# A spectral mixer with two MLP layers: the transforms of three of four batches on quarters of the array, and new places for the operands

## The chip, the core and the metric

One core of a Trainium2 chip (trn2). A time is the device time of one execution in microseconds (us); the kernel before took 1374.87 us, the median of three runs (1373.92 to 1375.44). A profile is one execution taken by the hardware profiler.

## The reference

Four batches of 3136 tokens with 256 features pass through three stages (`x` float32, everything in float32):

```
X = rfft(x, axis=tokens);  y = irfft(X * (filt_r + 1j*filt_i))          # a global filter
m = real(fft(fft(y, axis=tokens), axis=features)); u = y + m            # Fourier mixing
un = (u - mean(u)) / sqrt(var(u) + 1e-6)
v = u + max(un @ w_ch1, 0) @ w_ch2                                      # layer 1, 256 -> 1024 -> 256
vn = (v - mean(v)) / sqrt(var(v) + 1e-6) * g_ln
out = v + max(vn @ w_ch1', 0) @ w_ch2'                                  # layer 2
```

## The kernel before, in words

**Transforms.** 3136 = 64 x 49, so a transform over tokens is one over 64 (index p) and one over 49 (index q), without twiddle factors. `over_p(b)` (L346) multiplies the tokens of a batch by the 64-point matrix `f1`: a chunk holds two blocks of 256 features, a block holds two q of 64 p, and `f1` is block-diagonal, 128 x 128. The products (64 real numbers per q: 32 frequencies, real and imaginary) go to DRAM (`g_dram`). `over_q(b)` (L393) reads them back with q and real/imaginary on 98 partitions, two of the 33 frequencies per step (17 steps, `XCH`), multiplies by the 49-point matrix `f2` (128 columns), multiplies by the filter (L455 to L463, with real and imaginary halves on partitions 0 to 63 and 64 to 127), goes back with `i1` (L475), and stores to `v_dram`. On the way it makes the spectrum of the filtered signal (`z`, L498) and transposes it (L479); from it comes the mixing term. `prep_ticks(U)` (L561) makes a unit U of four tiles of 128 tokens: the mixing (L592) and the last 64-point product `i2` (L606) accumulate in one bank, even and odd parts apart, and `token` (L594) makes sum and difference.

**Exact and split products.** The matrix engine has two ways here. An exact product takes float32 operands (L309). A split product (`mm3`, L219) uses float32r operands, each split into a high and a low part (ScalarE makes the high part, L224, GpSimd or VectorE the low one, L225), in three passes. Before, batch one, the first eight chunks (`N1`) of `over_p(1)` and unit 0 are exact; the rest of the transforms, the mixing and the layers are split.

**Layers.** `w1_step` (L761) multiplies 128 of the 1024 hidden features (six matmuls of 512 columns; weights stationary, `xt` moving), `w1_evict` (L776) makes `hh` and `hl` from the bank, `w2_step` (L788) accumulates the second product (twelve matmuls of 256 columns; `hh`, `hl` stationary, weights moving). A block is eight such steps of one unit and layer, 50 blocks are 400 steps.

**Order.** The order is written out by hand: each generator (`over_p`, `over_q`, `prep_ticks`, `ln_ticks`, `conv_ticks`) yields ticks, and a table puts ticks at steps of the layers (`at`, `PAIRS`, `P1`, `CONV`). An engine executes its instructions in program order. The main loop (L988 to L999) does `w1_step` of two steps ahead, the ticks of this step, `w2_step`, `w1_evict`. Batch one is transformed ahead of the first layer step (`DURING`, `AFTER`), together with the decoding of the weights (`conv_ticks`) and the first part of batch two. SP issues nearly all loads, ScalarE the stores of `g_dram` and `v_dram`. PSUM has 8 banks of 128 x 512 in one pool.

**Places.** Tiles of a pool lie one behind the other in SBUF, rounded up to 32 bytes a partition, pools in the order in which they are made (L161 to L181).

Of the kernel before, what the change touches and what calls it, by code (L numbers as in the profile page):

```python
# [9 lines left out]
F32 = mybir.dt.float32  # L10
# [9 lines left out]
NP, NQ = 64, 49  # L20
# [3 lines left out]
NV = 4 * NH  # L24
NJ = 25
KK = [0, 32] + list(range(1, 32))
NK = len(KK)
NT = B * S // 128
NU = 6 * B


CN = ["f1", "f2", "f2a", "f2b", "i1", "i1a", "i1b", "i2", "cs0", "cs0b", "cs1", "cs1b", "id"]
CI = {n: i * 128 for i, n in enumerate(CN)}
NCONST = len(CN) * 128 + 2 + NK + D + 128

# [13 lines left out]
def _consts():  # L49
    c = np.zeros((128, NCONST))  # L50
    p = np.arange(NP)
# [5 lines left out]
    f1 = np.zeros((NP, 2, 32))  # L57
    f1[:, 0, :] = c64[:, :32]
    f1[:, 1, 1:] = -s64[:, 1:32]
    f1[:, 1, 0] = c64[:, 32]  # L60
    f1 = f1.reshape(NP, 64)
# [6 lines left out]
    for h in range(2):  # L68
        r = slice(64 * h, 64 * h + 64)
        c[r, CI["f1"] + 64 * h:CI["f1"] + 64 * h + 64] = f1  # L70
        c[r, CI["i2"] + 64 * h:CI["i2"] + 64 * h + 64] = i2


# [9 lines left out]
    for n, m in (("f2", f2), ("f2a", f2a), ("f2b", f2b)):  # L83
        c[:98, CI[n]:CI[n] + 128] = m.reshape(98, 128)


    h49 = slice(0, NH)
    i1 = np.zeros((2, 64, 2, NH, 2))
    i1[0, :NQ, 0, :, 0] = c49[:, h49]
    i1[0, :NQ, 0, :, 1] = s49[:, h49]  # L90
    i1[1, :NQ, 1, :, 0] = -s49[:, h49]
    i1[1, :NQ, 1, :, 1] = c49[:, h49]
# [5 lines left out]
    for n, m in (("i1", i1), ("i1a", i1a), ("i1b", i1b)):  # L98
        c[:, CI[n]:CI[n] + NV] = m.reshape(128, NV)

# [7 lines left out]
    c[:, CI["cs0"]:CI["cs0"] + 256] = cs0  # L108
    c[:, CI["cs1"]:CI["cs1"] + 256] = cs1
    c[:, CI["id"]:CI["id"] + 128] = np.eye(128)  # L110

    o = len(CN) * 128
    c[:64, o] = 1.0
    c[64:, o] = -1.0
    c[0, o + 1] = 1.0
    c[1:, o + 1] = -1.0
    k = _crt()[np.array(KK)]
    sg = np.where(k == 0, 0, np.where(k < S // 2, 1, np.where(k == S // 2, 0, -1)))

    f2s = -f2[:, :, ::-1]  # L120
    c[:98, NCONST - 128:] = f2s.reshape(98, 128)
    c[:NQ, o + 2:o + 2 + NK] = sg.T
    c[64:64 + NQ, o + 2:o + 2 + NK] = -sg.T
    for r in (0, 64):
        c[r, o + 2 + NK:o + 2 + NK + D] = np.where(e % 2, -1, 1)
    return c.astype(np.float32)

NA, LAG = 3, 3  # L130
N1 = 8
AHEAD = 3
# [939 lines left out]
```

## Time and profile before

| | |
|---|---|
| median of three runs | 1374.87 us |
| span of the profiled execution, first to last instruction | 1372.8 us |
| what lies around the span, against the median | 2.1 us |
| TensorE matmul busy | 1346.0 us, 98% |
| VectorE, ScalarE, GpSimd busy | 890.3, 746.7, 411.0 us |
| DMA | 157.06 MB, mean 114 GB/s |

The profile gives no time of its own for the profiled execution beside its span; the span stands for it. PE is the matrix engine (TensorE) and PEld its weight load, DVE is VectorE, ACT ScalarE, POOL GpSimd, SP the engine that issues DMAs. L221 is line 221 of the kernel. Matmuls are pipelined: a record's duration includes the time through the array, and the distance from one start to the next is shorter. An exact matmul instruction leaves two records, a split pass one.

### The profile page before, as it was taken

The page shows a single profiled execution, that of the slowest core. Times are in us where ns is not written, and L with a number is a line of the kernel's source. Part 1 is how long each engine was busy: PE and PEld are TensorE (multiplying, and loading weights), DVE is VectorE, ACT ScalarE, POOL GpSimd, SP SyncE. Part 2 cuts the span into 40 slices and gives each one's busy share as a digit, 9 for nine tenths or more (in the row PEclk, how much of TensorE's full clock was granted, in tenths as well). Part 3 has the DMA queues.
Part 4 walks back from the last instruction along what each step waited for, and adds up shares of the span by engine and source line. Part 5 has one row for each costly group of instructions (what it writes and reads, how often), then busy time and mean ns, then how long its engine had stood idle before and what let it go on. Part 6 is the DMA issues. An engine that isn't in the chain of part 4 may idle for free.

```text
span 1372.8 us, 23348 instructions
## 1 busy us (share of the span) xinstructions
PE 1346.0 (98%) x8619; PEld 1192.2 (87%) x8619; DVE 890.3 (65%) x1742; ACT 746.7 (54%) x1529; POOL 411.0 (30%) x358
## 2 busy tenths in 40 slices
PE   8978999999999999999999999999999999999998
PEld 6547898888889989898899998898999999999998
DVE  5978887787555767877554667678555555555353
ACT  5665555666555665656446556566534444454322
POOL 1742134545332433534043344344111101101000
PEclk9999999999999999999999999999999999999999
DMA  8872324354435534624544544445222413422200
GB/s 303 283 227 100 102 82 120 119 154 118 133 110 146 151 87 136 179 68 121 121 129 126 144 114 144 111 134 131 65 62 47 92 32 70 85 78 46 62 16 24
DMA packets 224338, 157.06 MB, mean 114 GB/s; under 512 B 164352, under 2 KB 187904, under 8 KB 224224
## 3 DMA queue, kind: packets, MB, share of 16 engines
q1 hardware_dynamic: 208272, 132.37, 35.0%
q10 hardware_dynamic: 15952, 23.20, 5.3%
q8 instruction: 68, 1.11, 0.3%
q14 instruction: 46, 0.38, 0.1%
HBM read 99.83 MB, written 55.71 MB: 113 GB/s over the span
## 4 chain that ended last, share of the span: by engine, by line
PE 87%; DVE 6%; ACT 2%; DMA 2%; issue 2%; POOL 1%; SPq 0%; ACTq 0%; DVEq 0%; POOLq 0%
PE ps L799 36%; PE ps L771 36%; PE ps L221 8%; PE ps L592 2%; PE ps L309 1%; DVE t L460 1%; PE ps L326 1%; DVE xtl L690 1%; PE ps L479 1%; DVE y L455 1%; POOL y L462 1%; PE ps L447 1%; DVE hl L782 1%; DVE nb L648 0%; PE ps L696 0%
## 5 line engine op out<-in xcount | busy, mean ns | idle before, releaser
L782 DVE SCALAR_TENSOR_TENSOR hl<-ps,hh 128x512 fp32r<-128x512 f32 (+1 forms) x400 | 270.4, 677 | 286.2 <-ACT hh L781 281.5
L781 ACT ACTIVATE hh<-ps 128x512 fp32r<-128x512 f32 (+1 forms) x400 | 232.9, 585 | 325.0 <-PE ps L799 310.5
L771 PE MATMUL ps<-xth,w1a 128*128 128x512 f32 (+1 forms) x800 | 244.6, 387 | 0.0
L771 PE MATMUL ps<-xth,w1b 128*128 128x512 f32 (+1 forms) x800 | 243.8, 386 | 0.0
L799 PEld LDWEIGHTS ps<-w2b,hh 128*128 128x128 f32 x1568 | 208.9, 188 | 13.2
L799 PE MATMUL ps<-w2a,hh 128*128 128x256 f32 x1568 | 217.0, 281 | 0.4 <-ACT hh L781 0.4
L799 PE MATMUL ps<-w2b,hh 128*128 128x256 f32 x1568 | 217.0, 281 | 0.0
L799 PEld LDWEIGHTS ps<-w2a,hh 128*128 128x128 f32 x1568 | 206.9, 189 | 11.4 <-ACT hh L781 0.9
L644 POOL TENSOR_TENSOR rs<-rs,mhalf 128x4 f32<-128x4 f32 (+1 forms) x51 | 50.7, 994 | 376.3 <-DVE rs L643 263.5
L771 PE MATMUL ps<-xtl,w1a 128*128 128x512 f32 (+1 forms) x400 | 156.5, 391 | 2.0 <-DVE xtl L690 2.0
L771 PE MATMUL ps<-xtl,w1b 128*128 128x512 f32 (+1 forms) x400 | 155.8, 390 | 0.2 <-DVE xtl L699 0.2
L771 PEld LDWEIGHTS ps<-xth,w1a 128*128 128x128 f32 x800 | 135.7, 188 | 17.2 <-ACT xth L224 0.2
L771 PEld LDWEIGHTS ps<-xth,w1b 128*128 128x128 f32 x800 | 135.2, 188 | 16.5
L655 ACT ACTIVATE xn<-u,nb,rs 128x256 f32<-128x256 f32 x152 | 120.0, 839 | 53.0 <-DVE nb L648 53.0
L462 POOL TENSOR_TENSOR y<-y,t 128x512 f32<-128x512 f32 (+1 forms) x67 | 98.3, 1467 | 144.4 <-DVE t L460 112.4
L799 PE MATMUL ps<-w2b,hl 128*128 128x256 f32 x784 | 122.4, 277 | 1.2 <-DVE hl L782 1.2
L799 PE MATMUL ps<-w2a,hl 128*128 128x256 f32 x784 | 122.5, 278 | 1.1 <-DVE hl L782 1.1
L799 PEld LDWEIGHTS ps<-w2b,hl 128*128 128x128 f32 x784 | 103.9, 188 | 2.0 <-DVE hl L782 2.0
L799 PEld LDWEIGHTS ps<-w2a,hl 128*128 128x128 f32 x784 | 104.4, 189 | 1.3 <-DVE hl L782 1.3
L225 POOL TENSOR_TENSOR sl<-gr,sh 98x512 fp32r<-98x512 f32 x48 | 62.1, 1294 | 141.5 <-ACT sh L224 141.5
L803 DVE TENSOR_TENSOR u<-ps,u 128x512 f32<-128x512 f32 x98 | 63.2, 686 | 46.7 <-PE ps L799 46.7
L771 PEld LDWEIGHTS ps<-xtl,w1a 128*128 128x128 f32 x400 | 75.3, 188 | 19.0 <-DVE xtl L690 4.1
(132 smaller groups left out, 2053.8 us busy)
## 6 DMA issues: line engine op xcount, KB each, us to landing
fc<-in_ff SPq DMA_DIRECT2D x61, 512.0 KB
xd<-xn SPq DMA_DIRECT2D x38, 512.0 KB
xtl<-xd SPq DMA_DIRECT2D x152, 128.0 KB
vd<-vst ACTq DMA_DIRECT2D x64, 200.0 KB
xr<-in_x SPq DMA_DIRECT2D x48, 256.0 KB
vr<-vd SPq DMA_DIRECT2D x48, 256.0 KB
out<-u SPq DMA_DIRECT2D x24, 512.0 KB
gr<-gd SPq DMA_DIRECT2D x48, 196.0 KB
```

What stands on the lines that cost most here:

```text
L221: nc.tensor.matmul(out=o, lhsT=lhs[a], rhs=rhs[b], start=start and i == 0, stop=stop and i == 2)
L225: (lo_eng or nc.vector).tensor_tensor(out=lo, in0=src, in1=f32(hi), op=ALU.subtract)
L309: nc.tensor.matmul(out=o, lhsT=cf[i // 512][:k, i % 512:i % 512 + w], rhs=rhs[:k, c0:c1], start=start, stop=stop)
L462: (nc.gpsimd if b or t < n - 1 else nc.vector).tensor_tensor(out=y[:, :nk], in0=y[:, :nk], in1=t2[:, :nk], op=ALU.add)
L592: nc.tensor.matmul(out=o, lhsT=lhs, rhs=rhs[r], start=i == 0, stop=False)
L644: nc.gpsimd.tensor_tensor(out=rs[:, tl], in0=rs[:, tl], in1=mhalf[:, tl], op=ALU.pow)
L655: nc.scalar.activation(out=xs[t], in_=u[:, t].rearrange("p (k a j) -> p j k a", k=2, j=4), func=ACTF.Identity, scale=rs[:, t:t + 1], bias= ...
L771: nc.tensor.matmul(out=o, lhsT=w[:, a, k, m * 128:m * 128 + 128], rhs=xt[s][:, k, :n], start=i == 0, stop=i == 5)
L781: nc.scalar.activation(out=h[:, :n], in_=ps[:, :n], func=ACTF.Relu)
L782: nc.vector.scalar_tensor_tensor(out=l[:, :n], in0=ps[:, :n], scalar=0.0, in1=f32(h[:, :n]), op0=ALU.max, op1=ALU.subtract)
L799: nc.tensor.matmul(out=o[:, t % 2], lhsT=a[:, t * 128:t * 128 + 128], rhs=w[:, b, m], start=m == 0 and i == 0 and t % 2 == 0, stop=m == 7 ...
L803: nc.vector.tensor_tensor(out=u[:, t - 1:t + 1], in0=o, in1=u[:, t - 1:t + 1], op=ALU.add)
```

## The change

1. Batches two to four are folded ahead: the host lays token block q and block 49 - q side by side, GpSimd makes their sum and difference (`fold`). The 49-point transforms then have 50 rows (25 cosine, 25 sine) and each product is one of a 64-row, 64-column quarter of the array, in exact float32 (`quarter`). Nothing of batches two to four is split any more, in `over_p`, `over_q` or the product `i2` of `prep_ticks`; the mixing and the layers stay split.
2. Real and imaginary parts lie in different banks (R, I), and the two halves of the partitions hold two frequencies, so the filter takes four multiplications and two GpSimd additions for four frequencies; the half spectrum `z` moves from VectorE to GpSimd. `over_q` has 9 double steps (`NDUO`) instead of 17, `over_p` 7 chunks instead of 13. The filter of these batches is loaded once per frequency and not twice; `v_dram` has 128 rows per frequency instead of 100.
3. Batch one keeps its full-array exact products, in a function of its own (`first_q`) with the same arithmetic. Of the constants only the cosines and sines of the mixing are split now.
4. The pools are put in another order with gaps (`PAD`, in words of 4 bytes) between them, so that the operands of the layers start at chosen places modulo 256 bytes.
5. The tables of ticks change (`DURING`, `AFTER`, `P1`, `PAIRS`); loads of x come in chunks of 512 KB.

```
+PAD = (24, 16, 56, 40, 16, 8, 40)
-PAIRS = [(4, 5), (10, 11), (0, 1), (2, 3), (12, 14), (6, 8)]
+PAIRS = [(6, 7), (12, 13), (1, 2), (10, 11), (14, 15), (3, 5)]
...
+    sm = pool("sm", 4)
+    head = pool("head", 1)
+    gap("gap0", PAD[0])
     keep = pool("keep", 1)
+    gap("gap1", PAD[1])
+    keep64 = pool("keep64", 1)
+    uop = pool("uop", 1)
+    gap("gap2", PAD[2])
+    wp1 = pool("wp1", 1)
+    gap("gap3", PAD[3])
+    wp2 = pool("wp2", 1)
...
+    gap("gap5", PAD[5])
     xtp = pool("xtp", 2)
+    gap("gap6", PAD[6])
     hp = pool("hp", 2)
...
+    def quarter(o, c, lhs, r, k, rhs, **kw):
+        nc.tensor.matmul(out=o[c:c + 64], lhsT=lhs[r:r + k], rhs=rhs[r:r + k], **{"start": True, "stop": True, **kw})
...
+    def fold(b, c, minus):
+        t = x_raw.pop((b, c))
+        if c == 6:
+            return t
+        xf = raw.tile([128, 2, 2, D], F32, tag="xf", name="xf")
+        nc.gpsimd.tensor_tensor(out=xf[:, 0], in0=t[:, 0::2], in1=t[:, 1::2], op=ALU.add)
+        minus.tensor_tensor(out=xf[:, 1], in0=t[:, 0::2], in1=t[:, 1::2], op=ALU.subtract)
+        return xf
...
+    def over_p(b):
...
+        for c in range(7):
+            cur = xf
+            if c + 1 < 7:
+                xf = fold(b, c + 1, nc.gpsimd)
...
+                ps = [bank() for _ in range(2)]
+                for g in range(2):
+                    for h in range(2):
+                        quarter(ps[h], 64 * g, const("f1", 64 * g, 64), 64 * h, 64, flat(cur[:, g]))
...
+        def into(j):
+            g = g_raw.pop((b, j))
+            R, I = (bank(2) for _ in range(2))
...
+                n = len(steps_of(j))
+                for c in range(2):
+                    for r, o in ((0, R), (64, I)):
+                        quarter(o[:, :n], 64 * c, f2, r, NI, g[:, c:2 * n:2])
+        def filt(j, R, I):
...
+            for o, i, a in ((y[:, :n, 0], R, 0), (t2[:, :n, 1], R, 1), (y[:, :n, 1], I, 0), (t2[:, :n, 0], I, 1)):
+                nc.vector.tensor_tensor(out=o, in0=i[:, :n], in1=f[:, :n, a], op=ALU.mult)
+            nc.gpsimd.tensor_tensor(out=y[:, :n, 1], in0=y[:, :n, 1], in1=t2[:, :n, 1], op=ALU.add)
+            nc.gpsimd.tensor_tensor(out=y[:, :n, 0], in0=y[:, :n, 0], in1=t2[:, :n, 0], op=ALU.subtract)
+        def half(j):
...
+            for r, op in ((0, ALU.add), (1, ALU.subtract)):
+                eng.tensor_tensor(out=z[:, :n, r, 1:], in0=y[:, :n, r, 1:128], in1=y[:, :n, r, 129:], op=op)
+        def back(j):
...
+                for c in range(2):
+                    for h in range(2):
+                        quarter(V[h][:, :n], 64 * c, const("i1", 64 * c, 64), 64 * h, NQ, y[:, :n, c])
...
+        for j in range(NDUO + lag):
+            RI = into(j) if j < NDUO else None
+            if j >= lag:
+                back(j - lag)
+            if RI:
+                filt(j, *RI)
+            yield
+            if j >= lag:
+                turn_z(j - lag)
...
-            for a in range(2):
-                ps = bank(2)
-                for eo in (1, 0):
-                    mix(ps[:, eo], a, eo)
-                    mm3(ps[:, eo], con("i2"), cols(vs[eo], a * D, a * D + D), start=False)
...
+        for eo in (1, 0):
+            for a in range(2):
+                for h in range(2):
+                    quarter(ps[a][:, eo], 64 * (h ^ a), const("i2"), 64 * h, 64, vs[eo][:, a], start=False,
+                            stop=eo == 0, skip_group_check=True)
```

Three double steps differ from what is quoted: in the first (frequencies 0, 32 and 1) `into` has eight quarters of 256 columns and `back` six, in the last each has four of 256 columns; in `over_p` the seventh chunk has two quarters of 256 columns.

## Rows read from the trace of the kernel before

**Rows 1.** The page's header, busy times, and granted clock by slice of the span
```profile
span 1372.8 us, 23348 instructions
...
PE 1346.0 (98%) x8619; PEld 1192.2 (87%) x8619; DVE 890.3 (65%) x1742; ACT 746.7 (54%) x1529; POOL 411.0 (30%) x358
...
PEclk9999999999999999999999999999999999999999
```

**Rows 2.** The page's chain that ended last, shares of the span
```profile
PE 87%; DVE 6%; ACT 2%; DMA 2%; issue 2%; POOL 1%; SPq 0%; ACTq 0%; DVEq 0%; POOLq 0%
PE ps L799 36%; PE ps L771 36%; PE ps L221 8%; PE ps L592 2%; PE ps L309 1%; DVE t L460 1%; PE ps L326 1%; DVE xtl L690 1%; PE ps L479 1%; DVE y L455 1%; POOL y L462 1%; PE ps L447 1%; DVE hl L782 1%; DVE nb L648 0%; PE ps L696 0%
```

**Rows 3.** Waits of TensorE: total us, times, longest
```profile
PE ps L326 <- DMA xr<-in_x: 4.2, 1, 4.2
PE ps L696 <- ACT xn L661: 3.2, 6, 1.3
...
PE ps L771 <- DVE xtl L699: 0.2, 1, 0.2
```

**Rows 4.** Busy time by stretch (engines in the header line), all; then L221 alone
```profile
core 0: us, PE busy (x) PEld busy (x) DVE busy (x) ACT busy (x) POOL busy (x), PEclk, DMA share, GB/s
...
200.00:950.00 750.00, 747.69 (x4816) 670.75 (x4815) 509.58 (x961) 447.24 (x934) 290.46 (x245) 1.00 0.46 127
...
0.00:94.00 94.00, 0.00 (x0) 0.00 (x0) 1.00 0.78 270
...
200.00:950.00 750.00, 121.67 (x537) 87.51 (x537) 1.00 0.46 127
950.00:1372.00 422.00, 21.47 (x114) 16.61 (x114) 1.00 0.25 57
sum 1372.00, PE 153.86 PEld 112.30; mean PE 38.47 PEld 28.07
```

**Rows 5.** Timeline of TensorE: start, duration, instructions; split products, then a layer step
```profile
611.24 0.40 PE L221 MATMUL ps<-sh,chi 98*128 98x512 f32 x1
...
612.42 0.39 PE L221 MATMUL ps<-sl,chi 128*100 128x512 f32 x1
612.65 0.38 PE L479 MATMUL ps<-ctail,z 128*128 128x128 f32 x2
...
614.24 0.62 PE L771 MATMUL ps<-xth,w1b 128*128 128x512 f32 x2
...
615.62 0.28 PE L799 MATMUL ps<-w2b,hh 128*128 128x256 f32 x1
```

**Rows 6.** Timeline of TensorE, a unit's mixing and last transform
```profile
635.41 0.28 PE L592 MATMUL ps<-chi,zsh 128*128 128x256 f32 x1
...
636.83 1.07 PE L799 MATMUL ps<-w2a,hh 128*128 128x256 f32 x8
```

**Rows 7.** Timeline of TensorE, exact products of batch one
```profile
36.83 1.02 PE L447 MATMUL ps<-gr,f2s 98*128 98x512 f32 x2
37.69 1.02 PE L309 MATMUL ps<-y,cr 128*100 128x512 f32 x2
38.55 0.38 PE L479 MATMUL ps<-ctail,z 128*128 128x128 f32 x2
```

**Rows 8.** Groups by form of TensorE: count, busy us, mean ns, idle before
```profile
L221 PE MATMUL ps<-sl,chi 128*128 128x256 f32 x99 | 28.1, 284 | 1.8 <-DVE sl L225 1.8
...
L221 PE MATMUL ps<-sh,chi 128*100 128x512 f32 x45 | 18.1, 401 | 0.0
...
L221 PE MATMUL ps<-sh,chi 128*128 128x512 f32 x28 | 11.4, 407 | 0.0
...
L309 PE MATMUL ps<-xr,cr 128*128 128x512 f32 x16 | 7.9, 597 | 1.1 <-DMA xr<-in_x 1.1
L221 PE MATMUL ps<-sl,chi 98*128 98x256 f32 x9 | 2.5, 283 | 0.0
```

**Rows 9.** Timeline of TensorE, two layer steps late in the span
```profile
1202.44 1.09 PE L799 MATMUL ps<-w2a,hh 128*128 128x256 f32 x8
```

**Rows 10.** Groups by form: splits and additions on GpSimd and ScalarE
```profile
L462 POOL TENSOR_TENSOR y<-y,t 128x512 f32<-128x512 f32 x63 | 95.1, 1509 | 142.2 <-DVE t L460 112.4 <-ACT xth L685 15.5 <-DVE t L457 9.8
...
L225 POOL TENSOR_TENSOR sl<-gr,sh 98x512 fp32r<-98x512 f32 x48 | 62.1, 1294 | 141.5 <-ACT sh L224 141.5
...
L224 ACT ACTIVATE sh<-gr 98x512 fp32r<-98x512 f32 x48 | 29.9, 622 | 0.0
```

**Rows 11.** Groups by form: the filter's products and the half spectrum on VectorE
```profile
L460 DVE TENSOR_TENSOR t<-ps,fc 64x512 f32<-64x512 f32 x98 | 67.5, 688 | 1.3
...
L498 DVE SCALAR_TENSOR_TENSOR z<-y,ctail 128x254 f32<-128x254 f32 x64 | 52.0, 814 | 0.1
```

**Rows 12.** The chain in order of time, 0 to 100 us: start, us, what
```profile
55.30 5.62 DMA fc<-in_ff
60.94 6.05 DMA ww<-in_w2a
```

More of the change, by code (lines that the diff above doesn't have):

```diff
@@ L67, in _consts @@
     i2 = i2.reshape(64, NP) / NP
[L68 to L71, printed above, removed]
+    for h in (0, 64):
+        for g in range(2):
+            put("f1", h, f1[g], 64 * g)
+        put("F1", h, f1[0], h)
+        put("i2", h, i2)
+    n = np.arange(NH)
+    cc, ss, z = np.zeros((3, 2 * NH, NQ))
+    cc[2 * n] = c49[n]
+    ss[2 * n + 1] = s49[n]
+    ss[1] = 0
+    put("f2", 0, cc + ss)
+    put("f2", 64, cc - ss)
+    put("f2a", 0, cc)
+    put("f2a", 64, -ss)
+    put("f2b", 0, -ss)
+    put("f2b", 64, cc)
     f2 = np.zeros((NQ, 2, 2, 64))
@@ L82, in _consts @@
     f2b[:, 1] = f2[:, 0]
[L83 to L92, printed above, removed]
+    for name, m in (("F2", f2), ("F2a", f2a), ("F2b", f2b), ("F2s", -f2[:, :, ::-1])):
+        put(name, 0, m.reshape(98, 128))
+    qs = np.array(QPOS)
+    i1 = np.zeros((2, NQ, NH, 2))
+    i1[0, :, :, 0] = c49[:, qs]
+    i1[0, :, :, 1] = s49[:, qs]
+    i1[1, :, :, 0] = -s49[:, qs]
+    i1[1, :, :, 1] = c49[:, qs]
     i1 /= NQ
@@ L296, in spectral_mlp_kernel @@
-    cf, turned = {}, {}
-    def operand(exact, src):
-        if not exact:
-            return split_tiles(src, nc.gpsimd)
-        return src.rearrange("p a d -> p (a d)")
-    def product(exact, o, name, rhs, c0, c1, w=128, k=128, start=True, stop=True):
-        if not exact:
-            mm3(o, con(name, w, k), cols(rhs, c0, c1, k), start, stop)
-        else:
-            i = CI[name]
-            assert i // 512 in cf
-            nc.tensor.matmul(out=o, lhsT=cf[i // 512][:k, i % 512:i % 512 + w], rhs=rhs[:k, c0:c1],
-                             start=start, stop=stop)
+        nc.sync.dma_start(out=t[:, :nk], in_=ff0[:, k0:k1])
@@ L422, in over_q @@
+        for i in range(2, AHEAD):
+            load_f0(i)
         yield
-        gs[0] = operand(b == 0, g_raw.pop((b, 0)))
-        sign(0)
+        f = f_sb[0, 0][1]
+        for a in range(2):
+            nc.scalar.activation(out=f[:, a], in_=f[:, a], func=ACTF.Copy, scale=sg0[:, a:a + 1])
         yield
@@ L585, in prep_ticks, with token @@
              for a in range(2)]
-        def mix(o, a, eo):
-            rhs = con("cs1" if eo else "cs0", 256)
-            for i, (s, r) in enumerate(PASSES):
-                lhs = zmid[:, 128 * a:128 * a + 128] if eo == 0 and i == 2 else z[a][eo][s]
-                nc.tensor.matmul(out=o, lhsT=lhs, rhs=rhs[r], start=i == 0, stop=False)
-        def token(even, odd, a):
+        cs = [{"h": chi[:, 256 * e:256 * e + 256], "l": clo[:, 256 * e:256 * e + 256]} for e in range(2)]
+        if U:
+            yield
+        ps = [bank(2) for _ in range(2)]
+        for a in range(2):
+            for eo in (1, 0):
+                for i, (s, r) in enumerate(PASSES):
+                    lhs = zmid[:, 128 * a:128 * a + 128] if eo == 0 and i == 2 else z[a][eo][s]
+                    nc.tensor.matmul(out=ps[a][:, eo], lhsT=lhs, rhs=cs[eo][r], start=eo == 1 and i == 0, stop=False,
+                                     skip_group_check=True)
+        if not U:
+            yield
+        def token(a):
+            even, odd = ps[a][:, 0], ps[a][:, 1]
             uo = uop.tile([128, D], F32, tag="uo", name="uo")
@@ L878, in spectral_mlp_kernel @@
             "c": lambda: run(cw, 1),
[L879 to L881 removed]
+            "k": lambda: cf.update({2: temp("hl", CS["cs0"][0], 512)}),
+            "s": cosines,
             "f": lambda: run(p1, 1),
```

630 lines of the change are left out of this document (351 added, 279 removed).

## The prediction

> **What bounds the kernel now.** I read the page's header and engine shares first, then the chain that ended last, then the stages, then the starts of single matmuls. TensorE is busy for 1346.0 of 1372.8 us at a granted clock of 9 tenths or more in every slice, and VectorE, the next one, for 890.3 [rows 1]. A busy share alone says little here, because the records overlap: a record lasts 392 ns where the next begins 235 ns later. So I looked at what ends waits. The chain runs over TensorE for 87% of the span; the two layers hold 36% each, the split products of the transforms (L221) 8% [rows 2]. All waits of TensorE for another engine that the view lists come to some 20 us, and the largest single one, 4.2 us, is the first load [rows 3]. By stage, TensorE is busy 747.7 of 750 us between 200 and 950 us, and L221 lies there for 121.7 of its 153.9 us; after 950 us only 21.5 us of it are left, and before 94 us none [rows 4]. From 94 us on the time is thus the sum of the matmuls' start-to-start distances, and the change is priced by the columns that it takes out of that queue and puts into it. The other engines matter only if one of them comes to be late.
>
> **Prices.** Of the split (float32r) products, seven starts with 512 columns lie between 611.24 and 612.65: 0.235 us each [rows 5]. Twelve with 256 columns between 635.41 and 636.83: 0.118 us each [rows 6]. An exact float32 product leaves two records: four of them with 512 columns lie between 36.83 and 38.55, 0.43 us each, so 0.86 us for one product [rows 7]. At 256 columns I take half, 0.215 a record.
>
> **What goes.** L221 has 45 x 6 + 28 x 3 = 354 records of 512 columns and 99 x 3 + 9 x 6 = 351 of 256 [rows 8]. 354 x 0.235 = 83.2, 351 x 0.118 = 41.4. The exact first eight chunks of batch two go too: 16 records [rows 8] x 0.43 = 6.9. Together **131.5 us** of TensorE's queue.
>
> **What comes.** Every one of these products becomes exact float32 on a 64 x 64 quarter. The counts are from the diff. Per batch `over_p` has 24 quarters of 512 columns and 2 of 256; `into` 28 and 12; `back` 28 and 10. Three batches: 240 and 72. `prep_ticks` has 8 of 256 columns for each of 24 units: 192. (Unit 0 was exact before and has as many records; it is left out on both sides.) So 240 quarters of 2 x 0.43 us and 264 of 2 x 0.215 us: 206.4 + 113.5 = **320 us if they run one after another**. Four quarters cover the whole array. If four at once take the time of one full product, it is **80 us**. No row shows two matmuls that use different parts of the array; every row of before is of 98 rows or more and 98 columns or more. So the two bounds for the pure products are 80 - 131.5 = -52 us and 320 - 131.5 = +188 us. The point from which the edit loses is an overlap of 320 / 131.5 = 2.4.
>
> I take the four-fold end, with a price for entering and leaving. Each tick writes its quarters in an order that never repeats a quarter within four instructions, to two pairs of banks, and the nearest rows show that TensorE begins a matmul while the one before is still in flight (0.40 us of duration against 0.235 of distance), so what it lacks for overlap is a free part of the array, which the quarters give. The price: around a group of quarters the array changes from whole-array work and back. No row shows it; from below it is nothing, and from above I take the depth of the pipeline twice: a layer matmul of 256 columns lasts 0.28 us and eight of them take 1.09, so the distance is (1.09 - 0.28) / 7 = 0.116 and 0.28 - 0.116 = 0.163 us are still in flight [rows 9]. Groups per batch: 7 in `over_p`, 10 ticks with `into` and `back` next to each other; three batches 51, and 24 units: 75. 75 x 2 x 0.163 = 24.5 us. I take it whole, since the weights of four quarters must be loaded before all four can run and no cheaper row exists. Net: 131.5 - 80 - 24.5 = **27 us less**.
>
> The Trainium skill, "TensorEngine Tiling (Array Packing)", section Tiling Modes, says that tiles work independently and in parallel, and that changing the tiling mode drains TensorE. By its first half alone the sum would be -52 us; its second half speaks against so many small groups, and with a drain at each end it is the -27. No row of this trace shows either half.
>
> **What lies beside.** The splits of batches two to four and of units 1 on leave ScalarE (48 + 48 + 48 + 28 at some 0.62 us, about 107 us) and GpSimd (48, 48, 42 and 28 at 1.3 us, 219 us) [rows 10]. GpSimd gets instead 36 halves of a fold, 54 adds of the filter and 54 half-spectrum adds, at 1.5 us each at most [rows 10], so at most 216; with the 48 adds of y that also go (72 us) it has less to do. VectorE has 27 steps of four products of 512 columns at 0.69 (74 us) for 51 steps of three such products and a z of 0.81 (147 us) [rows 11]. DMA loads half the filter. None of this is on the path; if a fold came late, TensorE would stand for one addition, 1.5 us, at some of 21 places. The filter's four products at 0.69 put 2.75 us on VectorE's queue before the next `hl`, where 2.06 stood; two steps of 2.76 us lie between an eviction and its use, so I cost it at nothing. Each tick takes four banks where three were, and I found no step that then lacks one for more than the eviction of a pair, 1.2 us.
>
> **The first 94 us.** This stage is no queue of matmuls: the chain passes through a filter load (5.62 us) and a weight load (6.05 us) at 55 to 67 us [rows 12]. The change has one split of constants there instead of three, loads weights later, and adds folds. Bounds: -12 us, if both loads leave the chain, to +6, four folds in the way; I take 0.
>
> **The places modulo 256 bytes.** Tiles are laid one after another, so the starts follow from the sizes in the code: w1 96 and x 160, w2 96 and h 160 before; w1 32 and x 96, w2 192 and h 0 after. The distance of moving to stationary operand stays what it was: 64 for the first layer product and -64 for the second. That the distance is what counts is suggested by two neighbours: L221 stands at a distance of 128 and needs 0.235 us for 512 columns, the first layer product at 64 needs 1.38 / 6 = 0.230 [rows 5]. I take 0. Bounds: 400 steps of 18 matmuls; at L221's price the first product would lose 400 x 6 x 0.005 = 12 us, with the second (12 x 0.002 x 400) 22 us; a gain of the same size below.
>
> The sum is -27 us, all of it from TensorE's queue. Page and median differ by 2.1 us (1372.8 and 1374.87), about the size of what a measurement of this kernel can tell from no change, 0.2% or 2.7 us; I subtract from the median: **1348 us**.
>
> **Rivals.**
> *Two in flight, not four.* Each exact product is two records, one behind the other, of the same quarter [rows 7]. If matmuls begin in order, the second record waits for the first and everything behind it waits too; then only the second record of one quarter runs beside the first of the next. A quarter costs one record plus one more per group: 240 x 0.43 + 264 x 0.215 = 160, and for the ends 18 x 0.43 + 3 x 0.215 + 30 x 0.43 + 24 x 0.215 = 26: 186, plus up to 24.5. That is 186 - 131.5 = +54 to +79 us: **1429 to 1454**, slower. It decides from an overlap below 2.4, or 3.0 with the ends paid. For it: all records of the trace start in the order of the program. Against it: nothing in a row, as no row has two quarters. The Trainium skill, "TensorE: Matmul & The Clock Gate", Part 3, says that matmuls start and end strictly in program order, which is this rival; by it the time is the one just given.
> *In order in each half of the rows.* If the two halves of the rows have queues of their own, four quarters take three records' times in a lone group: 240 / 2 x 0.43 + 264 / 2 x 0.215 + 26 = 106, so -25 us, with the ends 0: **1350 to 1375**. The rows speak for it as little as against it.
> *Units stay pairs.* In `prep_ticks` two quarters of different rows write one bank. If they shut each other out, 24 units x 4 x 0.215 = 21 us come back: **1369**.
> *No overlap.* +188 to +213: **1563 to 1588**. This is also the case in which the change does not do what it says.
> *The places do more or less than nothing.* The forecast with -22 or +22: **1326 or 1370**, and a layer that runs at 0.237 a matmul would end near 1378.
>
> **How the numbers follow.** Forecast 0.55, with its own range of 1323 (no price for the ends) to 1362. In-order halves 0.10, units as pairs 0.07, places 0.08, two in flight 0.15, no overlap 0.05. The range reaches from 1314 (the lower end, with part of the early stage's or the places' gain) to 1395, and leaves out the two slow cases. Faster: 0.55 + 0.08 of the halves + 0.05 of the pairs + 0.03 of the places = 0.71; within 0.2%: 0.02 of each of these three = 0.06; slower: 0.15 + 0.05 + 0.03 of the places = 0.23.
>
> **What would show it.** Four records of quarters beginning within some tens of ns of each other, and a group of four 512-column quarters that hands over to the next group after 0.86 us, show the overlap; starts 0.43 us apart show the second rival, 0.86 us the last. The first layer record behind a group, against its usual 0.230, shows the price of the ends. Layer matmuls still at 0.230 and 0.116 us show that the places do nothing. GpSimd below 411 us and TensorE's waits still near 20 us show that the rest stays hidden. The forecast is wrong if L799 and L771 move by over 1%, or if TensorE waits for z, y or xf in the middle of the span.

## The result, and the profile after

The kernel after takes **1360.47 us** (median of four runs, 1360.12 to 1361.03) against 1375.15 for the kernel before, timed beside it: a ratio of 0.9895, 95% interval 0.9881 to 0.9909, or 14.7 us less. The forecast was 1348 with a range of 1314 to 1395: the sign and the mechanism of the transforms are right, and the gain is little more than half of what was forecast. The spans differ by as much as the medians: 1372.8 and 1358.4 us, 14.4 us.

The page of the kernel after, the lines that answer to [rows 1] and [rows 2] (span, busy time and instructions, granted clock by slice, shares of the chain by engine and by line):

```profile
span 1358.4 us, 23128 instructions
...
PE 1331.0 (98%) x8917; PEld 1114.0 (82%) x8917; DVE 797.2 (59%) x1643; ACT 616.3 (45%) x1205; POOL 269.7 (20%) x277
...
PEclk9969999999999999999999999999999999999999
...
PE 89%; DVE 5%; DMA 2%; issue 1%; ACT 1%; POOL 1%; SPq 1%; ACTq 0%; POOLq 0%; DVEq 0%
PE ps L934 38%; PE ps L906 37%; PE ps L267 7%; PE ps L731 2%; PE ps L320 2%; DMA xr<-in_x 1%; PE ps L365 1%; PE ps L426 1%; PE ps L618 1%; DVE xtl L825 1%; PE ps L831 1%; DVE hl L917 1%; SPq L815 1%; PE ps L382 0%; DVE bs L775 0%
```

(L906 and L934 are the two layer products now, L267 the quarters, L731 the mixing, L618 the transposes of z in batches two to four.) TensorE is still the bound. There are 298 more matmul records and the engine is busy 15 us less. VectorE fell by 93 us, ScalarE by 130, GpSimd by 141; little of this can be on the chain, which ran over the three for 9% of the span before and runs over them for 7% now. One thing is new: the third character of the clock's row is a 6, and the stretch behind it is taken apart below.

**Do four quarters run at once?** First the timeline of TensorE around a step with two groups of four (start, duration, instructions):

```profile
606.28 0.63 PE L906 MATMUL ps<-xth,w1b 128*128 128x512 f32 x2
...
607.76 1.09 PE L267 MATMUL ps<-gr,con 50*64 50x512 f32 x8
608.67 1.04 PE L267 MATMUL ps<-y,con 49*64 49x512 f32 x8
609.64 1.20 PE L934 MATMUL ps<-w2b,hh 128*128 128x256 f32 x8
...
611.14 0.40 PE L906 MATMUL ps<-xth,w1b 128*128 128x512 f32 x1
```

Then the number of L267's records that are in flight in short stretches of the same time (the second bracket of a row counts the weight loads):

```profile
core 0: us, PE busy (x) PEld busy (x), PEclk, DMA share, GB/s
607.75:607.77 0.02, 0.01 (x1) 0.01 (x1) 1.00 0.00 0
607.77:607.78 0.01, 0.01 (x3) 0.01 (x3) 1.00 0.00 0
607.78:607.79 0.01, 0.01 (x4) 0.01 (x4) 1.00 0.00 0
607.79:608.24 0.45, 0.45 (x4) 0.18 (x8) 1.00 0.00 0
608.24:608.27 0.03, 0.03 (x8) 0.02 (x4) 1.00 0.00 0
```

By 607.79 the first records of all four quarters have begun, within 0.03 us. Then nothing begins for 0.45 us, about one record's time [rows 7], and between 608.24 and 608.27 four more begin, which I read as the second records of the same quarters: by the unrounded starts each begins 0.48 us behind the one at its place among the first four (607.765 and 608.245, 607.784 and 608.265). Eight records of 512 columns give way to the next eight after 608.67 - 607.76 = 0.91 us, where eight in single file need 3.4. The overlap is four-fold.

**Does one bank shut two rows of the array out?** A unit, where two quarters of different rows write one bank:

```profile
1231.42 1.09 PE L267 MATMUL ps<-vr,con 64*64 64x256 f32 x16
1232.45 1.20 PE L934 MATMUL ps<-w2a,hh 128*128 128x256 f32 x8
```

Sixteen records in 1.03 us from the first to what follows. Two groups of four need 4 x 0.215 = 0.86 us, eight pairs 1.72: they run four at a time here too.

**Plain layer steps.** Starts of the first layer product eight steps apart, with no other work between, after:

```profile
1143.47 0.40 PE L906 MATMUL ps<-xth,w1b 128*128 128x512 f32 x1
...
1165.44 0.40 PE L906 MATMUL ps<-xth,w1a 128*128 128x512 f32 x1
```

and before:

```profile
1062.99 0.39 PE L771 MATMUL ps<-xth,w1b 128*128 128x512 f32 x1
...
1085.07 0.39 PE L771 MATMUL ps<-xth,w1a 128*128 128x512 f32 x1
```

21.97 / 8 = 2.747 us a step, against 22.08 / 8 = 2.760. Over 391 steps that is 5.1 us. The same layer code with operands at other places runs 0.5% faster.

**The beginning.** The first layer matmul, after:

```profile
102.22 1.06 PE L906 MATMUL ps<-xth,w1a 128*128 128x512 f32 x2
```

and before, with the last of the exact chunks of batch two directly ahead of it:

```profile
93.39 1.02 PE L309 MATMUL ps<-xr,cr 128*128 128x512 f32 x2
93.85 1.02 PE L771 MATMUL ps<-xth,w1a 128*128 128x512 f32 x2
```

That is 8.4 us later. Busy times and granted clock by stretches of 10 us, after:

```profile
80.00:90.00 10.00, 5.35 (x29) 3.34 (x32) 5.01 (x9) 6.36 (x14) 3.86 (x4) 0.62 0.57 170
90.00:100.00 10.00, 7.07 (x32) 2.54 (x24) 4.88 (x16) 4.36 (x9) 7.83 (x8) 0.50 0.69 224
```

and before:

```profile
80.00:90.00 10.00, 6.54 (x26) 3.97 (x26) 7.54 (x20) 5.20 (x12) 6.40 (x6) 1.00 1.00 318
90.00:100.00 10.00, 8.03 (x38) 5.62 (x37) 5.06 (x13) 7.96 (x18) 3.17 (x3) 1.00 0.76 237
```

(Columns after the length: TensorE, its weight load, VectorE, ScalarE, GpSimd, then the clock.) TensorE is busy for less of the time, and the clock falls to 0.50, the lower of its two levels (1.2 GHz); from 70 to 80 us the engine had been busy for 6.14 us, where before it was busy for 6.74. The chain in order of time says what the engine waits for:

```profile
68.17 1.99 POOL y L437
70.16 1.69 POOL xf L333
...
71.89 3.24 PE ps L267 x8
...
78.83 3.89 DMA gd<-gst
...
82.79 0.61 ACT vst L461
...
86.48 2.97 DMA vr<-vd
```

An addition and a fold on GpSimd stand in line, then the store of `v` waits for a staging buffer that a store of `g` holds (78.83 to 82.72), and the first unit's load `vr` begins at 86.48; before, that load began at 80.85.

**What stays hidden.** Waits of TensorE, total, times, longest, come to 22.8 us, near 20 as before [rows 3]; the largest, and the one for a fold:

```profile
PE ps L831 <- ACT xn L796: 5.0, 6, 2.1
...
PE ps L267 <- POOL xf L333: 2.7, 3, 1.7
```

Two of these three waits lie ahead of the first layer matmul (71.9 and 91.9 us), the third, 0.6 us, is at 685.7. The view leaves out waits inside a group of quarters. At 372 us the second half of a fold is late (its load landed late, GpSimd waits for it), and one four takes 2.25 us instead of 1.09:

```profile
372.04 2.25 PE L267 MATMUL ps<-xf,con 64*64 64x512 f32 x8
```

The two steps with these late folds last 5.15 and 5.84 us where the other eight with one fold's four last 3.99: **3.0 us** in all. This is the wait for xf in the middle of the span that the prediction gave as a sign of being wrong; it is there, and small.

### The profile page after: what moved, and what is told of

The parts are those of the page before. It is cut to its first block, busy times and chain, and to the rows that moved or that the text cites. A ratio compares the mean times of both kernels' runs of the same rounds, so it can differ in the third digit from the quotient of the medians.

```text
span 1358.4 us, 23128 instructions
## 1 busy us (share of the span) xinstructions
PE 1331.0 (98%) x8917; PEld 1114.0 (82%) x8917; DVE 797.2 (59%) x1643; ACT 616.3 (45%) x1205; POOL 269.7 (20%) x277
## 4 chain that ended last, share of the span: by engine, by line
PE 89%; DVE 5%; DMA 2%; issue 1%; ACT 1%; POOL 1%; SPq 1%; ACTq 0%; POOLq 0%; DVEq 0%
PE ps L934 38%; PE ps L906 37%; PE ps L267 7%; PE ps L731 2%; PE ps L320 2%; DMA xr<-in_x 1%; PE ps L365 1%; PE ps L426 1%; PE ps L618 1%; DVE xtl L825 1%; PE ps L831 1%; DVE hl L917 1%; SPq L815 1%; PE ps L382 0%; DVE bs L775 0%
## 5 line engine op out<-in xcount | busy, mean ns | idle before, releaser
L906 PE MATMUL ps<-xth,w1a 128*128 128x512 f32 (+1 forms) x800 | 246.3, 390 | 0.0
L906 PE MATMUL ps<-xth,w1b 128*128 128x512 f32 (+1 forms) x800 | 245.4, 388 | 0.0
L934 PEld LDWEIGHTS ps<-w2a,hh 128*128 128x128 f32 x1568 | 203.9, 188 | 36.9 <-issue 24.5
L934 PEld LDWEIGHTS ps<-w2b,hh 128*128 128x128 f32 x1568 | 204.9, 188 | 27.4 <-issue 14.1
L934 PE MATMUL ps<-w2a,hh 128*128 128x256 f32 x1568 | 219.9, 282 | 0.0
L934 PE MATMUL ps<-w2b,hh 128*128 128x256 f32 x1568 | 216.0, 280 | 0.4 <-ACT hh L916 0.2
L906 PE MATMUL ps<-xtl,w1a 128*128 128x512 f32 (+1 forms) x400 | 156.0, 390 | 0.3 <-DVE xtl L825 0.3
L906 PE MATMUL ps<-xtl,w1b 128*128 128x512 f32 (+1 forms) x400 | 155.5, 389 | 0.0
L906 PEld LDWEIGHTS ps<-xth,w1a 128*128 128x128 f32 x800 | 136.6, 189 | 18.2 <-issue 1.6
L906 PEld LDWEIGHTS ps<-xth,w1b 128*128 128x128 f32 x800 | 135.7, 188 | 16.3
L934 PE MATMUL ps<-w2a,hl 128*128 128x256 f32 x784 | 123.4, 279 | 1.1 <-DVE hl L917 1.1
L934 PE MATMUL ps<-w2b,hl 128*128 128x256 f32 x784 | 123.3, 278 | 1.1 <-DVE hl L917 0.9
L934 PEld LDWEIGHTS ps<-w2b,hl 128*128 128x128 f32 x784 | 104.1, 188 | 1.9 <-DVE hl L917 1.9
L934 PEld LDWEIGHTS ps<-w2a,hl 128*128 128x128 f32 x784 | 104.5, 189 | 1.3 <-DVE hl L917 1.3
L906 PEld LDWEIGHTS ps<-xtl,w1a 128*128 128x128 f32 x400 | 75.3, 188 | 18.6 <-DVE xtl L825 1.4
L906 PEld LDWEIGHTS ps<-xtl,w1b 128*128 128x128 f32 x400 | 75.1, 188 | 17.7 <-DVE xtl L834 0.4
L775 DVE BATCH_NORM_STATS2 bs<-u 128x6 f32<-128x256 f32 x196 | 68.6, 412 | 0.0
```

The costliest lines, as they stand in the source:

```text
L775: nc.vector.bn_stats(out=st[:, t], in_=u[:, t])
L906: nc.tensor.matmul(out=o, lhsT=w[:, a, k, m * 128:m * 128 + 128], rhs=xt[s][:, k, :n], start=i == 0, stop=i == 5)
L934: nc.tensor.matmul(out=o[:, t % 2], lhsT=a[:, t * 128:t * 128 + 128], rhs=w[:, b, m], start=m == 0 and i == 0 and t % 2 == 0, stop=m == 7 ...
```

## The experiments

All times stand against the kernel before, timed beside them on the same chip (1374.86 to 1375.73), as a ratio with its 95% interval. Edits are to the kernel after unless said otherwise. No run takes the folding, the exact arithmetic and the packing by quarters apart from each other; what they are worth together is read from the steps of the traces. Starts of the first layer matmul need care: in four kernels whose code ahead of it is that of after (experiments 1, 2, 4 and 5) it starts at 103.7, 101.7, 102.8 and 104.6 us, so 1 or 2 us there cannot be told from nothing.

**1. places_before.** The gaps put the operands of the layers, and those of the mixing, back to the places that they had; the code stays.

```
-PAD = (24, 16, 56, 40, 16, 8, 40)
+PAD = (32, 8, 8, 64, 64, 64, 64)
```

> The changed kernel with gaps between the pools that put every operand back where it was modulo 256 bytes before the change (w1 96, x 160, w2 96, h 160; the mixing's cosines 32 and its spectrum 160). My theory (only the distance of moving to stationary operand counts, and it is the same): the layers' plain step stays at 2.747 us, the mixing's twelve matmuls lose some 0.03 us a unit, in all 1360.5 to 1361.5 us. The rival (the places gave the plain step its 0.013 us): the plain step is back at 2.760 us, and 400 of them cost 5 us: 1365 to 1366 us.

1367.32 us, 0.9941 (0.9927 to 0.9954): some 6 to 7 us of the 14.7 are gone, more than the rival named. Two speeds stand side by side in one run. Starts of the first layer product six steps apart, then eight steps apart later in the span:

```profile
985.00 0.62 PE L906 MATMUL ps<-xth,w1a 128*128 128x512 f32 x2
...
1001.57 0.62 PE L906 MATMUL ps<-xth,w1a 128*128 128x512 f32 x2
...
1155.64 0.63 PE L906 MATMUL ps<-xth,w1b 128*128 128x512 f32 x2
...
1178.09 0.63 PE L906 MATMUL ps<-xth,w1a 128*128 128x512 f32 x2
```

16.57 / 6 = 2.76 us, the step of the kernel before, and 22.45 / 8 = 2.81. At the old places a step can run in either pattern and keeps the one it is in: behind the eighth step there are 116 plain steps at 2.760, 123 at 2.806 and 16 at 2.781. All 123 follow a step with a unit's mixing and quarters, and none follows a fold's quarters, a tick of `over_q` or transposes. In the kernel before, where the last transform of a unit was split, there are 228 at 2.760 and 7 at 2.806, so the longer pattern goes with the unit's quarters: 123 x 0.046 = 5.7 us. At the new places there are 231 at 2.747 and 23 at 2.773.

**2. places_128.** The distance of moving to stationary operand is made 128 bytes.

```
+PAD = (24, 16, 56, 40, 16, 24, 40)
```

> The changed kernel with x and h moved so that moving and stationary operand of both layer products lie 128 bytes apart modulo 256 (64 and -64 in the changed kernel). If the distance counts, and at the price of the split products of the transforms of before, which lay at 128: six matmuls at 0.235 and twelve at 0.118 us make a plain step of 2.83 us instead of 2.747, 400 steps cost 33 us: 1390 to 1397 us. If places do nothing: 1360 to 1362 us.

1380.15 us, 1.0032 (1.0019 to 1.0045), with plain steps of 2.815 to 2.820: slower than before the change. The step came out near the 2.83 that was expected, the time did not reach 1390, as steps with quarters lost less (a tick 4.880 for 4.853). So the places alone span 20 us from the best of these to the worst.

**3. before_places.** The kernel before, with gaps that give its operands the new places.

```
+    gap("gap0", 48)
+    wp1 = pool("wp1", 1)
+    gap("gap1", 40)
+    wp2 = pool("wp2", 1)
...
+    gap("gap2", 16)
     zsp = pool("zsp", 1)
...
+    gap("gap3", 8)
     xtp = pool("xtp", 2)
+    gap("gap4", 40)
     hp = pool("hp", 2)
```

> The kernel before with gaps that give its layers the places of the changed kernel (w1 32, x 96, w2 192, h 0 modulo 256); its products stay split and whole. The first places kept two repeating layer steps in the kernel with quarters, of 2.760 and 2.806 us, and only the first in the kernel before. Theory (the places alone set the step): 2.747 us here too, 400 x 0.013 = 5 us less: 1369 to 1371 us. Rival (the places only keep the step out of the slow mode that a group of quarters leaves behind): the plain step stays at 2.760 us and the time at 1374 to 1376 us.

1374.32 us, 0.9995 (0.9986 to 1.0004): no gain. Its plain step is 2.747 (-5.1 us over 391 steps), but what stands between the steps takes 3.9 us more (half a unit's mixing with its last transform costs 1.471 us, where it cost 1.401), the first eight steps take 0.9 more, and the first layer matmul starts 0.4 us earlier. The spectrum and the cosines of the mixing moved against each other with the same gaps; that this is the cause was not tested. So the places are worth 5 us to the plain steps in either kernel, and in this one the time does not show it.

**4. split.** The backward product of a tick goes into the next tick, ahead of the transposes: one group of two fours becomes two groups of one. Behind the eighth step there are 90 groups for 66, so 24 more and not 27 (the first and the last tick of a batch have one product only).

```
             RI = into(j) if j < NDUO else None
-            if j >= lag:
-                back(j - lag)
...
             if j >= lag:
+                back(j - lag)
                 turn_z(j - lag)
```

> The changed kernel with the backward products of a step moved from behind the forward ones to the next tick, ahead of the transposes: the same matmuls in 27 groups of quarters more. Theory (a group costs 0.39 us for its ends whatever is in it): 27 x 0.33 to 0.39 us more, 1369 to 1371 us. Rival (the price goes with the number of quarters, or with their weight loads): no change, 1360 to 1361 us.

1364.87 us, 0.9929 (0.9915 to 0.9942), 4.4 us more than after. The timeline of two steps:

```profile
608.97 0.63 PE L905 MATMUL ps<-xth,w1b 128*128 128x512 f32 x2
...
610.45 1.09 PE L267 MATMUL ps<-gr,con 50*64 50x512 f32 x8
611.47 1.20 PE L933 MATMUL ps<-w2b,hh 128*128 128x256 f32 x8
...
612.96 0.63 PE L905 MATMUL ps<-xth,w1b 128*128 128x512 f32 x2
...
614.44 1.09 PE L267 MATMUL ps<-y,con 49*64 49x512 f32 x8
615.46 0.66 PE L618 MATMUL ps<-con,z 128*128 128x128 f32 x4
...
617.34 0.63 PE L905 MATMUL ps<-xth,w1a 128*128 128x512 f32 x2
```

With one four the step takes 612.96 - 608.97 = 3.99 us, 1.25 above a plain step; with two (the timeline of after, 606.28 to 611.14) 4.86, or 2.11 above. The difference, 0.86, is one four (0.86 by [rows 7]); what is left of 1.25, **0.39 us, is the price of the ends of a group**, paid once for one four or two. The group with transposes costs 617.34 - 612.96 = 4.38, 1.63 above plain, where a four alone and transposes alone (0.49) cost 1.74: beside quarters the transposes save 0.11. So a tick taken apart loses 0.28 us, 24 of them 6.7; the median rose by 4.4, and the rest lies in waits that this execution had less of (its late folds cost 0.8 us less, its plain steps 1.5).

**5. interleave.** Forward and backward product of one quarter next to each other, so that quarters repeat at once (the products are collected and issued in turn).

```
+            m2, m1 = held.pop(), held.pop()
+            for i in range(max(len(m1), len(m2))):
+                for m in (m1, m2):
+                    if i < len(m):
+                        m[i]()
```

> The changed kernel with the eight quarters of a tick of over_q in another order: each of the forward products is followed at once by the backward product of the same quarter, so that neighbours collide two by two. Theory A (a matmul that finds its quarter busy holds up all behind it): a tick needs about 10 passes of 0.43 us where it needed 4, 2.5 us more in some 24 ticks: 1415 to 1425 us. Theory B (each quarter has a queue of its own, or the passes are put in order beforehand): no change, 1360 to 1361 us. Between them, rows or columns with one queue each: 1375 to 1395 us.

1363.59 us, 0.9919 (0.9904 to 0.9935). The tick itself costs 4.873 us for 4.853: the order in which the kernel issues the quarters does not matter here, and Theory A is out. The records do not follow that order either. Forward and backward products (`gr`, `y`) alternate in the kernel, and in the trace all forward ones begin first:

```profile
488.96 1.11 PE L270 MATMUL ps<-gr,con 50*64 50x512 f32 x8
489.87 1.06 PE L270 MATMUL ps<-y,con 49*64 49x512 f32 x8
```

So a product that finds its quarter busy does not hold up the products of other quarters behind it. That speaks against the reason given for *two in flight*, and against the sentence ahead of the prediction that an engine executes its instructions in program order. Whether the chip or the building of the program puts them so (the two halves of Theory B) the trace does not show; the first four starts lie 13 ns apart where after has 6.5, as if each second product were passed over. Of the 3 us that this run takes more than after, 2.4 lie ahead of the first layer matmul (104.6 us), where the order of the products is unchanged; they were not traced to a cause.

**6. stage3.** A third staging buffer, so that the store of `v` need not wait for that of `g`.

```
-    stg = pool("stg", 2)
+    stg = pool("stg", 3)
```

> The changed kernel with three staging buffers for what is stored instead of two, nothing else. Theory: ahead of the first layer step a store of batch one waits from 80.8 to 82.8 us for a staging buffer that a store of batch two's first chunk holds; with a third buffer that wait goes and the first layer matmul comes 2 to 3 us earlier (102.2 us in the changed kernel): 1357 to 1359 us. Rival (the wait is covered by the decoding of the weights or by the next load): 1360 to 1361 us.

1359.36 us, 0.9886 (0.9873 to 0.9900), not to be told from after; the first layer matmul at 101.4, 0.8 us earlier, which is within the spread named above. The wait goes (the load of the first unit begins at 84.95 instead of 86.48), and little of it reaches the layers.

**7. late.** Two of batch two's ticks (`f`, a fold with its quarters) are taken out of the part before the layers and left to the layers.

```
-..., 34: 'c', 35: 'f', 37: 'f', 38: 'c'}
+..., 34: 'c', 38: 'c'}
```

> The changed kernel with the first fold, product and store of batch two taken out of batch one's last steps: two ticks fewer there, two more in the first layer steps. Theory: the fold on GpSimd (68 to 76 us) delays TensorE, VectorE and ScalarE's stores of batch one; without it the first layer matmul comes 5 to 8 us earlier than at 102.2 us, and the two ticks cost TensorE nothing later: 1353 to 1357 us. Rival (the clock is what is lost there, or the ticks are only late elsewhere): 1359 to 1362 us.

1359.64 us, 0.9884 (0.9871 to 0.9898). The first layer matmul comes 3.9 us earlier, at 98.3, and after eight steps 1.2 us are left of it. The chain of this run in the first layer steps:

```profile
102.20 1.31 DVE hl L917 x2
...
105.98 1.72 DVE wm L873
```

In the first steps VectorE decodes weights (`wm`) between the evictions (`hl`), and the chain runs over it. Coming earlier, the layers only meet VectorE.

**8. warm.** 28 unused float32r matmuls of 512 columns in TensorE's idle times, to keep the clock; they add work and change no result.

```
+        def warm(n):
+            ps = bank()
+            for i in range(n):
+                nc.tensor.matmul(out=ps, lhsT=chi[:, :128], rhs=clo, start=True, stop=True)
```

> The changed kernel with 28 matmuls of 512 columns that nothing reads, 8 and 20 of them in TensorE's idle times between 76 and 85 us. Theory: the granted clock there falls to half from 82 to 103 us (mean 0.62, 0.50 and 0.85 in three stretches of 10 us) because TensorE idles, and all that it has to do up to the first layer matmul takes twice as long; kept busy it stays at full clock and the first layer matmul comes 3 to 5 us earlier, 1356 to 1358 us. Rival (TensorE waits for loads and stores there, and its clock is hidden): 1360 us, or 1361 with the added matmuls in the way.

1357.74 us, 0.9875 (0.9862 to 0.9889), 2.7 us less than after, with intervals that overlap. The stretches again:

```profile
80.00:90.00 10.00, 10.00 (x64) 7.09 (x63) 6.06 (x9) 6.19 (x14) 4.32 (x5) 1.00 0.59 167
90.00:100.00 10.00, 5.56 (x27) 2.08 (x24) 6.08 (x19) 5.11 (x10) 8.54 (x8) 0.79 0.81 256
```

The clock is full from 80 to 90 and falls again once the unused work is over; the first layer matmul starts 1.2 us earlier, within the spread named above. So no more than a small part of the 8.4 us comes back with the clock, as far as this run held it. The gain of the median is not shown to be the clock's: the two profiled executions differ by 4.3 us, and 2.6 of these lie in the two steps in which after has a late fold.

**9. Combinations.** *best1* is warm and stage3, with two chunks of the forward transform of batches three and four in one tick and the transposes of z in the tick of the products. *best2* adds a unit's quarters ahead of its mixing and other `PAIRS`, so that nine ticks fall on the step of a unit's quarters. *best3* is best2 without the joined chunks, *best4* is best3 with late.

```
             if j >= lag:
                 back(j - lag)
...
-            yield
             if j >= lag:
                 turn_z(j - lag)
+            yield
...
-PAIRS = [(6, 7), (12, 13), (1, 2), (10, 11), (14, 15), (3, 5)]
+PAIRS = [(4, 6), (12, 13), (8, 9), (10, 11), (14, 15), (1, 2)]
```

> The changed kernel with four edits against what its profile and the runs showed: the 28 matmuls that keep the clock, a third staging buffer, the folds' chunks of batches three and four taken two by two (six groups of quarters fewer), and the transposes of z in the tick of the products instead of a step of their own. If a group costs 0.39 us and lone transposes 0.1 us more than beside quarters: 2.8 + 0 to 1.1 + 6 x 0.39 + 24 x 0.1 = 7.5 to 8.6 us less than the changed kernel, 1352 to 1353 us. Rival (five banks at once and larger chunks make TensorE wait for VectorE and ScalarE): the two later edits give nothing or lose, 1356 to 1360 us.

> As best1, with the unit's four-by-two quarters put ahead of its mixing, and the table of ticks changed so that about nine of the over_q ticks fall on the step of a unit's quarters and stand next to them: one group of quarters instead of two. Theory: 9 x 0.39 = 3.5 us less than best1. Rival (VectorE and ScalarE, with four filter products and a unit's sums in one step, come late with hh and hl): 1 to 5 us more than best1.

> Keeps of best2 the idle matmuls that hold the clock, the third staging buffer, the transposes of z in the tick of the quarter products, a unit's quarter products ahead of its mixing and the aligned pairs, and takes back the merging of the two chunks of the forward transform in batches three and four. Theory A: the merge is what cost best2 its gain (two batches of about 2.4 us each): without it the time is 1350 to 1353 us. Theory B: the two chunks cost the same in either place and the loss is elsewhere: 1355 to 1356 us, as best2.

> best3, and two of batch one's fold steps are left to the layers instead of standing before them. Theory A: the first layer matmul comes about 3 us earlier and the first eight steps give it back, as in the run that did this alone: the time is that of best3 within 1 us. Theory B: with the clock held, what was given back stays gained: 2 to 4 us less than best3.

best1 1356.07 (0.9855, 0.9839 to 0.9872), best2 1355.80 (0.9853, 0.9838 to 0.9867), best3 1356.22 (0.9857, 0.9841 to 0.9874), best4 1357.51 (0.9872, 0.9858 to 0.9887). The first three are one time within their intervals, some 4.5 us below after and 19 to 20 below before. None of the expectations below 1355 us came true; whether the chunks are joined makes no difference (theory B of best3), and late gives nothing, as in experiment 7 (best4 is 1.3 us above best3, with intervals that overlap). What they have over warm, 1.5 to 2 us, is within the intervals and less than the ends that they were to save. Two things are seen. In best1, TensorE waits 2.4 us for VectorE (`xn`) in the two steps where joined chunks meet the transposes of `xn`. And in best2 and best3 the quarters of a tick and of a unit do not stand next to each other: the transposes, which were moved into the tick, stand between them in eight of the nine steps. Best2:

```profile
313.55 1.09 PE L268 MATMUL ps<-gr,con 50*64 50x512 f32 x8
314.46 1.04 PE L268 MATMUL ps<-y,con 49*64 49x512 f32 x8
315.43 0.65 PE L656 MATMUL ps<-con,z 128*128 128x128 f32 x4
316.08 1.20 PE L268 MATMUL ps<-vr,con 64*64 64x256 f32 x16
```

A whole step of this kind costs 5.29 us above a plain one, where a tick with transposes (2.49) and a unit (2.64) apart cost 5.13: nothing is saved. In the ninth (201.31 us) there are no transposes, the two groups are one, and the step costs 3.52 for 1.25 + 2.64 = 3.89: 0.37 us less, the price of one group's ends. So the ends can be saved in this way, and the edit saved them once. The transposes themselves save 0.11 us a tick beside the quarters: 2.49 above a plain step, where after needs 2.11 and, in a later step, 0.49.

## Why the prediction was right, and where its sum was off

**The terms of the forecast, each with what it measured.** I split the difference of the spans by the starts of the layer steps, summed over the two traces.

| stretch | forecast | measured |
|---|---|---|
| to the first layer matmul, and the first eight steps | -1.5 | +8.37 - 2.64 = +5.7 |
| work between the steps, from the eighth on | -25.5 | -15.1 |
| plain steps (places) | 0 | -5.1 |
| sum | -27 | -14.4 |

The forecast's split: of the 131.5 us removed, 121.1 (345 x 0.235 + 339 x 0.118) lie behind the eighth step, of the quarters 432 records of 512 and 512 of 256, four at a time 74 us, and 66 groups x 0.327 = 21.6; 74 + 21.6 - 121.1 = -25.5. The rest is -1.5.

**What goes: right in the queue, wrong at its front.** The split products between the steps measured about 120 us (what their steps take above plain ones, less mixing and transposes) for the 121.1 priced. The 6.9 us of exact chunks were subtracted although all 16 records [rows 8] lie before the first layer matmul, the last two directly ahead of it: in a stretch of which the prediction itself said that it is no queue of matmuls. The quarters and ends of the same stretch were added at the same prices (6.0 and 2.9 us), so the fault all but cancels: without this stretch the sum is -25.5 instead of -27.

**What comes: the four-fold end was right,** count and all: L267 has 480 records of 512 columns and 544 of 256 (unit 0's 16 among them), and four quarters take 0.86 us. *Two in flight*, *in-order halves*, *units stay pairs* and *no overlap* fall with the rows above. The time alone would not decide it: 1360.47 lies in the range of *in-order halves* too, and what decides are the starts. The first of these rivals had matmuls begin in order, with a second record holding up all behind it; the counts in flight and experiment 5 show that it does not.

**The ends: the term was mis-sized,** 0.39 us measured for 0.327: 66 x 0.06 = 4.2 us. It is more than the 2 x 0.163 us that I took as a bound from above, so that was none. The Trainium skill, "TensorEngine Tiling (Array Packing)", section Tiling Modes, says that a change of tiling mode drains TensorE. The price paid once per group (experiment 4, 0.39 us) agrees with that; the drain itself is not seen, as the ends of matmul records are modelled. Two smaller losses stand beside it: the quarters between the steps cost 4.3 us more than fours and ends make (103.7 measured, 99.4 worked out), 3.0 of it in the two steps with late folds, which the prediction named and costed at nothing; and the transposes of z, which followed split products at 0.109 us each, now stand alone for the most part and cost 12.6 us for 10.8. Ends, quarters and transposes make 10.3 of the 10.4 us that are missing between the steps.

**The first 94 us: outside the bounds.** I had -12 to +6 and took 0; the first layer matmul came 8.4 us later. This term, taken at 0, is the one that failed most. The folds were named as a mechanism (+6) and are on the chain, but the sum missed what stands behind them there: the staging buffer, and the store and load of the first unit, each later than before; TensorE idles meanwhile and its clock falls. 5.6 of the 8.4 us are lost by the time that store is copied (`vst` at 82.79, before at 77.15), and 2.7 between the unit's load and the first layer matmul, with the clock at half. No single repair returns it: a buffer gives 0.8 us and the clock 1.2, both within the spread of this start, fewer folds give 3.9, and after eight steps 1.2 us are left of that. How the 8.4 divides between folds, staging and clock is open. The 2.6 us that come back in the first eight steps were not taken apart; each of the two traces has one short stretch of halved clock there (before near 110 us, after near 132).

**The places: right to keep as a rival, wrong to cost at nothing.** I argued from the distance of moving to stationary operand, which did not change; the step did, by 13 ns of 2760. The distance is then not all that counts. Experiments 1 to 3 show the effect alone: 5 us in the plain steps of either kernel, and 6 to 7 us in the time of this one, because at the old places a unit's quarters leave the steps in the longer pattern. Which pair of operands does it was not taken apart.

**What lies beside: right.** GpSimd is busy 269.7 us, below 411, ScalarE and VectorE fell by more than was counted (130 us for 107, 93 for 73), and TensorE's waits stayed near 20 us. No run shows that the 93, 130 and 141 us that VectorE, ScalarE and GpSimd lost bought anything by themselves.

Together: 10.4 us short between the steps, 7.2 at the beginning, 5.1 gained by the places: 27 - 10.4 - 7.2 + 5.1 = 14.5. That the time lies within the forecast's own range (1323 to 1362) is luck: without the 5.1 us of the places, which the sum had at nothing, it would be near 1365.6. The mechanism does not rest on that luck, since the work between the steps fell by 15.1 us without it.

## What to carry to other kernels

Products that fill a quarter of the array are worth packing by fours even in full float32, but each group costs its two ends, 0.39 us here: gather them behind one another, and look in the trace whether anything still stands between them. Price a saving only where the engine that gets it is the bound; a saving that lies ahead of the steady state is a saving for another sum. And when tiles are moved for any reason, measure a plain step of the inner loop first: it can change by 2.5% with nothing but the starting addresses.

## What the runs showed of the hardware that was not expected

The layer step repeats within 2 ns at one of a few lengths, 2.747, 2.760 or 2.806 us, and at one set of places at 2.815 to 2.820, set by the places of its operands. At one placement two lengths live side by side, and all 123 steps of the longer one follow a unit's mixing and quarters. The records of four exact products come in two rounds: four starts within 0.03 us, a pause of 0.45, four starts again, each 0.48 us behind its like in the first round. The same 0.48 us stand in experiment 5, where the starts of a round lie twice as far apart, and there the backward products begin 0.39 us behind the last start of the round before, less than the 0.43 us of a record: a record seems to wait for its own quarter and not for all four. And quarters overtake there: the product that the kernel issues second begins behind the one that it issues seventh (whether by the chip or by the building of the program is open).
